# A transformer block with its backward pass: transposes by DMA in place of TensorE, the first norm remade, statistics and affine steps on ScalarE, under a new instruction order

## The chip, the cores and the metric

The kernel runs on one core of a Trainium2 chip. The metric is the device time of one execution in microseconds (us). Three runs of the kernel before took 559.96, 557.95 and 559.55 us, median 559.55. Separately, one execution was profiled; its span, from the first to the last instruction, is 557.1 us.

## The reference

A pre-norm block on 2048 rows of 512 bfloat16 values: windowed attention (32 heads of 16, eight keys per query at distances 0, 2, ..., 14), a residual, a second norm, a feed-forward network of width 1792 with tanh-gelu, a residual. Output is the forward result and the gradients of seven inputs.

```python
qkv = (x @ wqkv)                      # norm(x) comes in as x
idx = pos[:, None] - off[None, :]     # off = 0, 2, ..., 14
logits = einsum("bhsd,bhswd->bhsw", q, k[idx]) * scale   # masked where idx < 0
o = einsum("bhsw,bhswd->bhsd", softmax(logits), v[idx])
h  = x + o @ wo
h2 = h + gelu(norm(h) @ w1 + b1) @ w2 + b2
# returned: h2, and vjp(grad_out) for x, wqkv, wo, w1, b1, w2, b2
```

## The kernel before

The 2048 rows are worked on in four chunks (c = 0 to 3) of 512 rows. Tiles are held in two layouts: token-major (rows on partitions) and feature-major (features on partitions); much of the work beside the matmuls is turning one into the other. TensorE can turn a 128x128 block with a matmul against an identity, whose result in PSUM must be evicted; the DMA engines can turn a whole 512x512 tile with a transposing transfer.

**Forward attention, per chunk** (`p1_ln` to `p1_h`). The first norm (`layernorm`, line 330) is taken, stored to DRAM (`ln1st`, line 579) and turned. q, k and v are projected; q and k come out feature-major. VectorE multiplies q with eight shifted k (`dots`, line 450), TensorE sums over a head, softmax follows. For the value sum, and later for the gradients, q, k, v and the gradient `go` must lie token-major in DRAM, so that a strided load, the *gather* (line 438, issued on GpSimd's queue), can fetch 18 neighbouring rows per partition. For k and q, `to_tm_store` (line 410) makes that copy: per half chunk, eight transposes on TensorE, one eviction by ScalarE, one store of 256 KB. `band` (line 487) multiplies gathered rows by coefficients on VectorE, sums on TensorE (line 502) and evicts on ScalarE (line 507), four times per chunk. Its token-major result is turned back by `turn` (line 511: eight transposes, one eviction; twice per chunk) or, for the pairs listed in `FMB` and `FMO`, by `turned` (line 522: one transposing DMA of 512 KB, from SBUF to SBUF). Then come `wo`, the residual (line 716), the second norm and its DMA turn.

**Feed-forward and its gradient, per chunk** (`p2_h`, `p2_out`, `p2_dg`, `p2_bwd`). 56 products of 4 matmuls per direction; ScalarE evicts and takes gelu, square and tanh, VectorE makes the gelu's derivative. The norm's gradient is `ln_bwd` (line 530): a scaled eviction with a sum on ScalarE, a reduction (line 539) and an affine step `u` (line 541) on VectorE, then two additions.

**Attention gradients, per chunk** (`p3_go`, `p3_dots`, `p3_bands` for q, v, k, `p3_gl1`). Three gathers and three bands per chunk; their results, turned, meet the transposed weights in `p3_gl1` (line 950), where the stored first norm is loaded again in permuted rows (line 941) for the norm's gradient. **Weight gradients** (`wg_ffn`, line 976) are matmuls over all rows, spread by the order over the second half as filler.

**What sets the order.** Each function registers operations through `op`, numbered as they are registered, with the buffers that they read and write. Nothing runs in that order: `emit` (line 118) issues the operations as the list `ORDER` (line 1182) says, by number, and each engine's program, SP's and GpSimd's DMA queues among them, is that list cut to the engine. An engine runs its program strictly in turn, so an instruction that waits holds all that stand behind it on the same engine. `HOMES` (line 1267) gives each buffer its SBUF address or PSUM bank. Two buffers at one address may not be live together, so a home adds waits too. Both lists were written by a planner ahead of time, which knew an estimated duration for each operation (the second argument of `op`).

## Time and profile before

| | before |
|---|---|
| median of three runs | 559.55 us |
| span of the profiled execution | 557.1 us |
| TensorE matmuls busy | 537.7 us (97%) |
| VectorE busy | 493.4 us (89%) |
| ScalarE busy | 314.7 us (57%) |
| GpSimd busy | 36.2 us (7%) |
| granted TensorE clock | 0.999 |
| moved by DMA | 126.65 MB, 227 GB/s in the mean |

The profiled execution's own time is not listed beside its span; the runs' median stands 2.45 us above the span.

A row that names a line, an engine and an operation gives the tile written and those read, the shapes, how often it ran (x64), then the busy time of the group, the mean of one in nanoseconds, and the engine's idle time ahead of it with what ended that. Busy time of TensorE merges overlapping matmuls, and each matmul's duration includes its way through the pipeline, so that the busy time of a short group is longer than what it delays the next. Rows of stretches ("82.00:196.00") give the length, then for PE (TensorE), PEld (its weight loads), DVE (VectorE), ACT (ScalarE) and POOL (GpSimd) the busy time and number of instructions, the granted clock, the mean busy share of the 16 DMA engines (which can exceed 1 when two queues interleave) and the bytes moved. In a row with a start, a duration and an engine, SPq is SP's DMA queue.

### The profile page before, as it was taken

To read this page: it belongs to the slowest core of one execution; us is meant where nothing else is said; L and a number is where in the kernel's file an instruction comes from. 1 tells how busy PE (TensorE), PEld (TensorE's weight loads), DVE (VectorE), ACT (ScalarE), POOL (GpSimd) and SP (SyncE) were. 2 spreads that over 40 slices of the span, in tenths; PEclk is the share of its full clock that TensorE was granted. 3 is DMA by queue.
4 is the path that set the end of the run, shared out by engine and by line. 5 is a ranking of instruction groups with operands and counts; after the bars stand their busy time and mean duration, and the time that the engine had idled before them with its cause. 6 is when DMAs were issued, how large, how long until landed. Compare 5 with 4: busy or idle time off the path is not lost. (4 is left out here: it accounts for less than half of the span.)

```text
span 557.1 us, 8572 instructions
## 1 busy us (share of the span) xinstructions
PE 537.7 (97%) x3276; PEld 248.1 (45%) x3327; DVE 493.4 (89%) x652; ACT 314.7 (57%) x500; POOL 36.2 (7%) x55
## 2 busy tenths in 40 slices
PE   7899899999999999999999999999999998999996
PEld 3454453444444444444444444464444443444442
DVE  7989999999999999787777378999999798999983
ACT  3997489978899956664440324122155534462423
POOL 1210010030000000002000000000011100010000
PEclk9999999999999999999999999999999999999999
DMA  8699979999688245589899988999999999887954
GB/s 253 180 276 269 350 199 375 259 224 284 172 210 241 62 122 132 114 167 244 161 201 187 204 170 188 247 222 245 197 328 286 390 264 377 287 339 165 243 126 130
DMA packets 199674, 126.65 MB, mean 227 GB/s; under 512 B 152081, under 2 KB 193233, under 8 KB 195537
## 3 DMA queue, kind: packets, MB, share of 16 engines
q1 hardware_dynamic: 194016, 84.68, 64.7%
q0 software_dynamic: 5616, 41.42, 20.1%
q8 instruction: 26, 0.43, 0.3%
q14 instruction: 16, 0.12, 0.1%
HBM read 55.74 MB, written 35.21 MB: 163 GB/s over the span
## 5 line engine op out<-in xcount | busy, mean ns | idle before, releaser
L823 PE MATMUL ps<-goT,w2T 128*128 128x512 bf16 x224 | 53.1, 379 | 0.4 <-DVE xb L825 0.2
L279 ACT CAST wgs<-ps 128x512 bf16<-128x512 f32 (+1 forms) x30 | 16.5, 563 | 64.8 <-PE ps L976 51.5
L741 PE MATMUL ps<-ln2T,w 128*128 128x512 bf16 x224 | 52.4, 379 | 0.2
L837 PE MATMUL ps<-w1T,xb 128*128 128x512 bf16 x219 | 50.9, 379 | 0.2
L795 PE MATMUL ps<-w,gl 128*128 128x512 bf16 x217 | 50.6, 379 | 0.4
L743 ACT ACTIVATE xb<-ps,b1c 128x512 bf16<-128x512 f32 x56 | 35.9, 693 | 19.1 <-PE ps L741 18.9
L950 PE MATMUL ps<-wqkvT,gqkvT 128*128 128x512 bf16 x186 | 44.1, 379 | 0.4 <-issue 0.2
L825 DVE SCALAR_TENSOR_TENSOR xb<-xb,ps 128x512 bf16<-128x512 bf16 x56 | 36.6, 682 | 7.3 <-PE ps L823 6.6
L976 PE MATMUL ps<-gor,gw2in 128*128 128x512 bf16 x164 | 39.2, 379 | 0.3 <-issue 0.2
L976 PE MATMUL ps<-gw1in,ln 128*128 128x512 bf16 (+1 forms) x185 | 38.9, 352 | 0.4
L493 DVE TENSOR_TENSOR prbk<-Rk,cfk 128x4096 bf16<-128x4096 bf16 x16 | 35.7, 2286 | 3.1 <-DMA Rk<-q_d 2.5
L493 DVE TENSOR_TENSOR prbq<-Rq,cfq 128x4096 bf16<-128x4096 bf16 x16 | 35.9, 2286 | 2.9 <-PE ps L502 2.0
L493 DVE TENSOR_TENSOR prbv<-Rv,cfv 128x4096 bf16<-128x4096 bf16 x16 | 35.7, 2280 | 2.9 <-DMA Rv<-go_d 2.0
L454 DVE TENSOR_TENSOR prb<-got,vw 128x4096 bf16<-128x4096 bf16 x16 | 36.0, 2273 | 1.6 <-ACT got L279 1.6
L493 DVE TENSOR_TENSOR prbo<-Ro,cfo 128x4096 bf16<-128x4096 bf16 x16 | 35.9, 2284 | 0.1
L454 DVE TENSOR_TENSOR prf<-qt,kt 128x4096 bf16<-128x4096 bf16 x16 | 35.9, 2277 | 0.0
L976 PEld LDWEIGHTS <-ln 128*128 128x128 bf16 x256 | 24.1, 98 | 25.2 <-issue 4.1
L823 PEld LDWEIGHTS <-w2T 128*128 128x128 bf16 x224 | 21.9, 98 | 27.4 <-issue 1.4
L837 PEld LDWEIGHTS <-xb 128*128 128x128 bf16 x224 | 21.9, 98 | 26.4
L795 PEld LDWEIGHTS <-gl 128*128 128x128 bf16 x224 | 21.8, 98 | 26.4 <-issue 0.4
L741 PEld LDWEIGHTS <-w 128*128 128x128 bf16 x224 | 21.4, 98 | 26.5 <-issue 2.5
L599 PE MATMUL ps<-ln1T,wqk 128*128 128x512 bf16 x127 | 30.0, 379 | 1.3 <-DMA wqk<-in_A_wqkv_dram 1.0
(174 smaller groups left out, 962.0 us busy)
## 6 DMA issues: line engine op xcount, KB each, us to landing
Ro<-v_d POOLq DMA_DIRECT2D x4, 1280.0 KB, 9.4
Rq<-k_d POOLq DMA_DIRECT2D x4, 1280.0 KB, 8.9
Rv<-go_d POOLq DMA_DIRECT2D x4, 1280.0 KB, 5.9
Rk<-q_d POOLq DMA_DIRECT2D x4, 1280.0 KB, 6.6
g_d<-gl SPq DMA_DIRECT2D x9, 512.0 KB, 3.7
gh_d<-xb SPq DMA_DIRECT2D x9, 512.0 KB, 4.2
Ro<-v_d POOLq DMA_DIRECT2D x4, 1024.0 KB, 7.3
Rq<-k_d POOLq DMA_DIRECT2D x4, 1024.0 KB, 8.3
```

Source lines behind the costliest of these rows:

```text
L279: fn = lambda: A.copy(out=ap(), in_=pap())
L454: op("DVE", tt_us(4096), lambda g=g, pr=pr: V.tensor_tensor(out=pr(), in0=ql()[:, g, :].unsqueeze(1).to_broadcast([P, W, 512]), in1=_sub(k ...
L493: V.tensor_tensor(out=pr().rearrange("p a j (d h) -> p a j d h", h=H), in0=_sub(R()[:, o0, 0:1], [[st, 2], [512, 4], [32, DH], [1, H]]), i ...
L599: T.matmul(ps()[:, gg * 512:(gg + 1) * 512], lhsT=wq_()[:, dc, sel * D + g * P:sel * D + (g + 1) * P], rhs=cols(st_[c]["ln1T"], dc, c in F ...
L741: T.matmul(ps(), lhsT=w1()[:, dc, f * P:(f + 1) * P], rhs=cols(ln2T[c], dc, c in FM2), start=(dc == 0), stop=(dc == DC - 1))
L743: op("ACT", act_us(512, 1), lambda f=f, ps=ps, xb=xb, f0=f0: A.activation(out=xb()[:, f - f0, :], in_=ps(), func=ACT.Identity, bias=b1c[:, ...
L795: T.matmul(ps(), lhsT=d["g"][f // 4]()[:, f % 4, j * P:(j + 1) * P], rhs=w2()[:, f, :], start=(f == 0), stop=(f == FT - 1))
L823: T.matmul(ps(), lhsT=w2T()[:, dc, f * P:(f + 1) * P], rhs=cols(goT, dc, True), start=(dc == 0), stop=(dc == DC - 1))
L825: op("DVE", 0.61, lambda f=f, ps=ps, z=z, f0=f0: V.scalar_tensor_tensor(out=z()[:, f - f0, :], in0=z()[:, f - f0, :], scalar=1.0, in1=ps() ...
L837: T.matmul(ps(), lhsT=d["d"][f // 4]()[:, f % 4, j * P:(j + 1) * P], rhs=w1T()[:, f, :], start=(f == 0), stop=(f == FT - 1))
L950: T.matmul(ps(), lhsT=gT()[:, j, b * P:(b + 1) * P], rhs=wqkvT()[:, k0 + b, :], start=(i == 0 and b == 0), stop=(i == 2 and b == 3))
L976: T.matmul(ps()[:, 0:N], lhsT=l, rhs=r, start=(n == 0), stop=(n == k - 1))
```

## The change

- **q and k copies** (`FMS = ("q", "k")`). `to_tm_store` is no longer called for them. `fm_store` writes each chunk feature-major to a new DRAM tensor (four stores of 128 KB). `fm_turn`, registered after the feed-forward's weights, reads it back by a transposing DMA and stores it token-major.
- **Turns** (`FMB` for all twelve, `FMO = (2, 3)`). The nine pairs that still used `turn` in the gradients (seven) and in the output of chunks 2 and 3 (two) use `turned`.
- **First norm** (`LX`). It isn't stored. In `p3_gl1` x is loaded in permuted rows and the norm is made again by 16 affine steps on ScalarE; for that the mean times the scale travels with the scale through the small DRAM detour (`rstdp` has twice the columns).
- **Second norm's statistics** (`S2A`). The residual add becomes an add with a running sum; per row tile ScalarE scales that sum and takes a square with a sum, in place of VectorE's two statistics instructions.
- **Norm gradients** (`UA`). `u` goes from VectorE to ScalarE.
- **`wo` transposed** (`WOD`). A DRAM-to-DRAM copy with permuted rows, then one transposing DMA, in place of a transposing DMA and a copy on GpSimd.
- Zero rows are stored from the warm-up's zero tile; two small memsets go.
- `ORDER` and `HOMES` are new throughout.

```diff
+    def fm_store(fm, off, n, c):
+        for g in range(4):
+            store(f_d[n][c], lambda g=g: _ap(f_t[n][c][8 * g:8 * g + 1, :], [[CH, 8], [H * CH, DH], [1, CH]]), fm, lambda g=g: fm()[:, g, off:off + CH], 128,
+                  key=g, skey=g // 2, tag="fst" + n)
+    def fm_turn(n, c, dst, back):
+        st = sb("ft" + n, [P, 4, D])
+        r = c * CH + (RPAD if back else 0)
+        xload(st, lambda: st(), lambda: f_t[n][c][:], 512, r=[f_d[n][c]], tag="fx" + n)
+        store(dst, lambda: dst()[r:r + CH, :].rearrange("(a p) d -> p a d", p=P), st, lambda: st(), 512, key=(c, 0), tag="tmst" + n)
...
+                if sq:
+                    jk = sb("jks", [P, D])
...
+                    op("ACT", 0.12, lambda t=t: A.mul(mv[:, t, 0:1], st[:, t, 0:1], -1.0 / D), r=[(ST, t)], w=[(MV, (t, 0))], tag="smean" + tag)
+                    op("ACT", act_us(D, 1, True), lambda t=t, j=j, jk=jk: A.activation(out=jk(), in_=src()[:, j, :], func=ACT.Square, bias=mv[:, t, 0:1],
+                                                                                       accum_out=mv[:, t, 1:2]),
...
-        store(ln1_d[c], lambda: ln1_d[c]()[:].rearrange("(j p) d -> p j d", p=P), ln1, lambda: ln1(), 512, tag="ln1st")
+        if not LX:
+            store(ln1_d[c], lambda: ln1_d[c]()[:].rearrange("(j p) d -> p j d", p=P), ln1, lambda: ln1(), 512, tag="ln1st")
...
+        if tag in UA:
+            op("ACT", act_us(D, 2), lambda: A.activation(out=u()[:, j, :], in_=xhap(), func=ACT.Identity, scale=sx_[:, i:i + 1], bias=c0_[:, i:i + 1]),
+               r=[xh, (SX, i), (C0, i)], w=[(u, j)], tag="u" + tag)
...
+            elif c in S2A:
+                op("DVE", 0.61, lambda j=j, ps=ps: V.tensor_tensor_reduce(out=h()[:, j, :], in0=ps(), in1=xt()[:, j, :], scale=1.0, scalar=0.0, op0=ALU.add,
+                                                                          op1=ALU.add, accum_out=st2[:, c * TPC + j, 0:1]),
...
+        if LX:
+            xr = sb("xr", [P, TPC, D])
...
+                op("ACT", act_us(D, 2), lambda t=t, j=j: A.activation(out=ln1()[:, j, :], in_=xr()[:, j, :], func=ACT.Identity,
+                                                                     scale=rstdp[:, t:t + 1], bias=rstdp[:, NT + t:NT + t + 1]), r=[xr, RP], w=[(ln1, j)], tag="nx")
...
+    if WOD:
+        op("SP", 0.5, lambda: SY.dma_start(out=wop_t[:], in_=_ap(A_wo, [[D, DH], [DH * D, H], [1, D]])), w=[WOP], dma=512 / DMA_RATE, tag="wop", mode=4)
...
-FMO = ()
-FMB = (('q', 3), ('v', 3), ('k', 3), ('k', 2), ('v', 2))
+FMO = (2, 3)
+FMB = tuple((n, c) for n in 'qvk' for c in range(4))
...
+FMS = ("q", "k")
+WOD = True
+LX = True
+S2A = (0, 1, 2, 3)
+S1A = ()
+UA = ("1", "2")
```

More of the change, by code (lines that the diff above doesn't have):

```diff
@@ L333, in layernorm @@
             acc = per == 1 and g0 in STA
+            sq = c in S2A if tag == "2" else per > 1 and c in S1A
             for j in js:
@@ L358, in layernorm @@
             else:
[L359 removed]
+                op("DVE", 0.08, lambda s=s, sq=sq: V.tensor_scalar(out=ve[:, s], in0=mv[:, s, 1], scalar1=1.0 / D if sq else EPS, scalar2=EPS if sq else None, op0=ALU.mult if sq else ALU.add,
+                                                                   **({"op1": ALU.add} if sq else {})),
                    r=[(MV, t) for t in ts], w=[(VE, k)], tag="ve" + tag)
@@ L646, in p1_qkv @@
         for fm, o, dd, back, n in ((kt, PAD, k_d, True, "k"), (qt, 0, q_d, False, "q")):
-            (tm_dma if (n, c) in TMD else to_tm_store)(fm, o, dd, c, back, n, c not in QKP)
+            if n in FMS:
+                fm_store(fm, o, n, c)
+            else:
+                (tm_dma if (n, c) in TMD else to_tm_store)(fm, o, dd, c, back, n, c not in QKP)
     def p1_attn(c):
```

79 lines of the change are left out of this document (51 added, 28 removed), and 240 rows, old and new, of tables (HOMES, ORDER).

## The prediction

> **What bounds the kernel now.** I read the page's first lines, then the busy time by stage, then the instructions around the first feed-forward matmul, then the chain that ended last.
>
> ```profile
> span 557.1 us, 8572 instructions
> ...
> PE 537.7 (97%) x3276; PEld 248.1 (45%) x3327; DVE 493.4 (89%) x652; ACT 314.7 (57%) x500; POOL 36.2 (7%) x55
> ```
>
> TensorE is nearly never idle, but the share is a mean. I cut the span where its character changes: the first feed-forward matmul (82), the end of the stretch with ScalarE full (196), the attention gradients under way (336), weight-gradient matmuls alone (546):
>
> ```profile
> core 0: us, PE busy (x) PEld busy (x) DVE busy (x) ACT busy (x) POOL busy (x), PEclk, DMA share, GB/s
> 0.00:82.00 82.00, 73.25 (x550) 36.00 (x558) 76.89 (x109) 60.04 (x82) 10.94 (x19) 1.00 0.87 256
> 82.00:196.00 114.00, 112.84 (x633) 50.97 (x641) 112.40 (x167) 106.84 (x135) 7.11 (x8) 1.00 0.84 229
> 196.00:336.00 140.00, 139.12 (x636) 63.21 (x646) 107.39 (x216) 63.83 (x111) 3.89 (x1) 1.00 0.83 170
> 336.00:546.00 210.00, 205.74 (x1432) 95.03 (x1454) 194.08 (x159) 82.27 (x171) 14.28 (x27) 1.00 0.89 260
> 546.00:557.10 11.10, 6.73 (x32) 2.84 (x29) 2.63 (x5) 1.76 (x4) 0.00 (x0) 0.94 0.41 118
> ```
>
> After 82 us TensorE is idle for 1.2 + 0.9 + 4.3 us before the tail: there the time is TensorE's stream, and only fewer matmul columns shorten it. The head is different. VectorE works 76.9 of 82 us, while TensorE has only projections and attention and leaves 8.8 us. What lets the feed-forward in is chunk 0's second norm:
>
> ```profile
> 72.88 0.15 DVE L364 SCALAR_TENSOR_TENSOR nm<-mv,rstd 128x4 f32<-128x4 f32 x1
> 73.14 2.93 ACT L369 ACTIVATE ln<-h,nm,rstd 128x512 bf16<-128x512 bf16 x4
> 76.09 1.89 SPq L273 DMA_TRANSPOSE ln2T<-ln  x1
> ...
> 81.92 0.81 PE L741 MATMUL ps<-ln2T,w 128*128 128x512 bf16 x3
> ```
>
> So VectorE's queue decides when `nm` comes (72.9), and the first feed-forward matmul follows 9 us later.
>
> **TensorE's part of the change.** All k and q transposes for the token-major copies (16 groups of 8) leave TensorE, and so do 18 `turn` groups: 14 of the gradients and 4 of chunks 2 and 3 of the attention output. That is 34 x 8 = 272 transposes. Their price is read from the chain, not from the groups' busy time:
>
> ```profile
> 478.49 0.89 PE ps L518 x16
> ...
> 543.23 9.51 PE ps L976 x44
> ```
>
> ```profile
> L419 PE MATMUL ps<-Pmat,kt 128*128 128x128 bf16 x64 | 4.9, 219 | 0.6 <-ACT tmv L279 0.6
> L419 PE MATMUL ps<-Pmat,qt 128*128 128x128 bf16 x64 | 4.7, 219 | 1.8 <-DVE h L716 1.0 <-ACT tmk L279 0.7
> ...
> L518 PE MATMUL ps<-ident,gqs 128*128 128x128 bf16 x48 | 3.7, 219 | 0.0
> ```
>
> Sixteen in a row move the chain 0.89 us, 0.0556 us each; the group's 0.075 us (4.9/64) holds a pipeline tail under which the next matmul already runs. 272 x 0.0556 = 15.1 us. Of these, the 128 k/q transposes all stand ahead of the first feed-forward matmul in the old order, so they lie in the head, and 144 (8.0 us) behind it. The new list also lets two band sums and one row sum (about 1.4 us) that stood ahead of that matmul come after it. So the stream behind it is shorter by 8.0 - 1.4 = 6.6 us. This saving is nearly certain if nothing else becomes the bound.
>
> **VectorE's and ScalarE's part.**
>
> ```profile
> L454 DVE TENSOR_TENSOR prf<-qt,kt 128x4096 bf16<-128x4096 bf16 x16 | 35.9, 2277 | 0.0
> ...
> L347 DVE BATCH_NORM_STATS2 st<-h 128x6 f32<-128x512 bf16 x16 | 10.8, 674 | 0.0
> ...
> L539 DVE CUSTOM_DVE_ANT_0 jk<-gyr,ln1b 128x512 bf16<-128x512 bf16 x16 | 10.7, 684 | 2.3 <-ACT gyr L536 2.3
> ...
> L716 DVE TENSOR_TENSOR h<-ps,xp 128x512 bf16<-128x512 f32 x16 | 10.5, 675 | 0.0
> ...
> L541 DVE TENSOR_SCALAR u<-ln1b,sx,c 128x512 bf16<-128x512 bf16 x16 | 6.3, 407 | 0.5
> ...
> L348 DVE BATCH_NORM_AGGREGATE mv<-st 128x2 f32<-128x6 f32 x32 | 5.8, 182 | 1.1
> ...
> L658 DVE TENSOR_REDUCE mx<-ps 128x128 bf16<-128x1024 f32 x4 | 4.8, 1208 | 0.0
> ...
> L676 DVE RECIPROCAL r<-ps 128x128 bf16<-128x128 f32 x4 | 3.7, 940 | 0.6 <-PE ps L671 0.6
> ```
>
> ```profile
> L279 ACT COPY gqkvT<-ps 128x1024 bf16<-128x1024 bf16 x14 | 14.1, 1014 | 7.9 <-PE ps L518 7.7
> L369 ACT ACTIVATE ln<-h,nm,rstd 128x512 bf16<-128x512 bf16 x16 | 11.9, 805 | 1.0 <-DVE nm L364 1.0
> L536 ACT ACTIVATE gyr<-ps,rstdp 128x512 bf16<-128x512 f32 x16 | 11.0, 687 | 22.9 <-PE ps L950 22.8
> ...
> L279 ACT COPY tmk<-ps 128x1024 bf16<-128x1024 bf16 x8 | 8.1, 1034 | 0.2 <-PE ps L419 0.2
> ...
> L538 ACT ACTIVATE c<-sg 128x1 f32<-128x1 f32 x32 | 5.9, 201 | 0.3
> ...
> L536 ACT ACTIVATION_READ_ACCUMULATOR gyr<-ps,rstdp 128x1 f32 x16 | 3.2, 198 | 0.0
> ```
>
> VectorE loses 16 x (0.674 + 0.182) = 13.7 us of second-norm statistics and 32 x 0.407 = 13.0 us of `u`. The residual add becomes an add with a sum; the nearest row with a sum is the custom reduction at 0.684, so +0.01 to +0.1 each. Net about -25 us. ScalarE loses 16 x 1.03 + 18 x 1.01 = 34.7 us of evictions. It gains 48 affine steps (32 `u`, 16 remade norms) x 0.805 = 38.6 us and 16 squares with a sum at 0.687 + 0.198 + 0.201 (the small scaling) = 1.09, so 17.4 us. Net +21, to 336 us, 62% of the span: no bound on the whole.
>
> In the head the list matters more than the sums. Counting what stands on VectorE ahead of chunk 0's `nm`: the old list has 12 products of q and k, 3 maxima, 3 reciprocals and 4 pairs of second-norm statistics; the new one 10, 1, 1 and none. That is 4.6 + 2.4 + 1.9 + 3.4 = 12.3 us, with the small ones about 13, so `nm` could come at 60 instead of 73. Against that, the new list puts a softmax exponent of chunk 2 on ScalarE between the first and the other three norms, and that exponent waits for a maximum that stands after `nm`. The head's gain lies between 0 and 13 us; I take 6.7, the middle, since the norm is released early and then partly held.
>
> **The DMA part.** Each k and q chunk goes out feature-major (4 stores of 128 KB in place of 2 of 256 KB), is read back transposed and stored again: 8 transposes and 8 stores of 512 KB more. 9 more `turned` transposes (2 for the output, 7 for gradients). 4 stores of the first norm go; its 16 loads become loads of x; the `wo` detour adds one copy and trades one transpose for another.
>
> ```profile
> 56.00:70.00 14.00, 12.31 (x130) 6.30 (x130) 13.90 (x17) 6.94 (x8) 0.54 (x1) 1.00 0.99 351
> ...
> 182.00:196.00 14.00, 13.87 (x64) 6.36 (x65) 13.73 (x26) 13.97 (x14) 1.03 (x1) 1.00 0.22 68
> 196.00:210.00 14.00, 13.70 (x63) 6.05 (x62) 13.86 (x28) 7.24 (x8) 0.00 (x0) 1.00 0.41 99
> 210.00:224.00 14.00, 13.95 (x66) 6.37 (x65) 13.90 (x29) 9.10 (x14) 0.00 (x0) 1.00 0.52 131
> 224.00:238.00 14.00, 13.95 (x66) 6.36 (x65) 11.05 (x18) 10.87 (x21) 0.00 (x0) 1.00 0.61 125
> 294.00:308.00 14.00, 13.95 (x65) 6.37 (x65) 10.45 (x32) 2.76 (x8) 0.00 (x0) 1.00 1.07 185
> ```
>
> The last of these windows holds nearly only transposes: 185 GB/s x 14 us = 2.59 MB, 4.9 of 512 KB, in 1.07 x 14 = 15 us of all engines, so 3.0 us each. The first holds plain traffic: 4.9 MB in 13.9 us, 1.5 us per 512 KB. The change adds 17 x 3.0 + 8 x 1.5 + 1.5 - 4 x 1.5 = 59 us of DMA. The k and q detour is 36 us of it; priced at 0.216 us a matmul (9.51/44), TensorE's stream in the new list stands at 124 to 200 us where they are issued, and in the old run the clock is some 28 us ahead of the stream (82 against 54 at the first feed-forward matmul). So it is the stretch from 152 to 228, whose last windows have 0.78 + 0.59 + 0.48 + 0.39 of 14 us free, 31 us; its readers, the k and q gathers, stand 110 us further on in the list. I cost it at nothing; without that cover it would press on the 0.83 to 0.89 of the later stages.
>
> The 7 gradient transposes add 21 us to the stage 336:546, whose DMA share is 0.89 x 210 = 187 us: 208 of about 203 us. That is over 1, yet 294:308 ran at 1.07 with TensorE busy 13.95 of 14. SP pays 1.9 us for each (the `ln2T` row), behind which it holds x loads, weight-gradient loads and stores; it has room:
>
> ```profile
> SPq L273 <- DVE prbv L493: 17.3, 1, 17.3
> ```
>
> The `wo` copy on GpSimd (3.9 us) falls in a stage with VectorE idle a quarter of the time: nothing.
>
> **Sum.** 557.1 - 6.6 (stream) - 6.7 (head) = 543.8 us of span. The median of the runs, 559.55, stands 2.45 above the profiled span, so 546 us.
>
> **The rivals.**
>
> Half the engines: each new k or q store walks its destination with an outermost size of 8. If a DMA is spread over no more engines than that, the 20 stores listed ahead of the first feed-forward matmul take 20 x 0.25 x 1.5 x 2 = 15 us on half the engines, which at the head's 0.87 have only 11 free; ln2's transpose then queues and the head stays: 557.1 - 6.6 + 2.45 = 553 us. For it: the head's windows reach 0.99. Against: the removed stores (8 of 256 KB and 4 of 512 KB) give back 12 us on all engines. [...] Chance 0.09.
>
> ScalarE bounds 82:196, where it works 106.8 of 114 us. The stage gains 12 squares (13 us) and about 4 `u` (3), and loses some 6 evictions (6): 117 us in a stage that should itself shrink. If gelus and evictions wait for that, it costs 3 to 8 us: about 552. Against: the next stage has ScalarE at 64 of 140, and its tanh and squares can be late. Chance 0.09.
>
> Gathers late, and slower than before: TensorE's one large gap in the last stage is a k band behind its gather.
>
> ```profile
> 472.50 0.61 PE L502 MATMUL ps<-prbk,S 128*32 128x512 bf16 x8 [1.73 <-DVE prbk L493]
> ```
>
> ```profile
> DVE prbk L493 <- DMA Rk<-q_d: 2.5, 2, 1.6
> ```
>
> With 21 us more of transposes on the engines that carry the gathers, each of the 12 q, v and k gathers could open such a gap: 12 x 1.73 = 21, so 546 + 21 = 567 us. From 7 such gaps on the result is no change, from 10 slower. Against: today only two waits of this kind exist, with windows over 1.0. Chance 0.14, 0.08 of it slower.
>
> The whole head gain: `nm` at 60 and nothing holds the norms: 557.1 - 6.6 - 13 + 2.45 = 540 us. Chance 0.12.
>
> [...]
>
> **How the numbers follow.** Forecast 0.56 (its own range 542 to 551), rivals 0.09, 0.09, 0.14, 0.12. The range 538.5 to 555 holds all but the late gathers and the edges. Within 0.5% (what a measurement of this kernel can't tell from no change) is 556.8 to 562.4. Faster 0.86, same 0.06, slower 0.08.
>
> **What would show it.** TensorE busy 520 to 524 us; no `tmk`, `tmq`, `gqkvT` evictions; first `ln2T` matmul at about 75 us (82: the head stayed; 69: all of it); DMA share above 0.5 in the stretch 150 to 230; no new gaps ahead of `prbk`, `prbv`, `prbq`. Wrong if TensorE's idle time after the first feed-forward matmul exceeds 20 us, or if ScalarE is full up to 200 us with TensorE waiting for `xb`.

## The result, and the profile after

The changed kernel took 554.15 us (median of 4 runs, 551.92 to 555.12); the kernel before, on the same chip, took 558.97 us (4 runs, 557.95 to 559.96). The ratio is 0.9908, 95% interval 0.9886 to 0.9930: faster by 0.9%, more than the 0.5% that the prediction takes for no change. The forecast was 546.0, with a range of 538.5 to 555.0. So the direction came true and the range held, but only 4.8 of the 13 us arrived. (Of the runs further down one, 557.99 us of x9, lies over 1.5% above that kernel's fastest and is left out of its ratio.)

The first lines of the page of the changed kernel: span, busy time, the granted clock in 40 slices, and SyncE's DMA queue.

```profile
span 553.3 us, 8162 instructions
...
PE 530.4 (96%) x3055; PEld 233.8 (42%) x3055; DVE 473.0 (85%) x606; ACT 334.3 (60%) x564; POOL 34.8 (6%) x54
...
PEclk8989999899999999999999999999999999999999
...
q1 hardware_dynamic: 232592, 96.26, 76.2%
```

VectorE lost 20.4 us (forecast 25) and ScalarE gained 19.6 (forecast 21). TensorE has 272 matmuls fewer by its weight loads (3327 before, 3055 now), as counted, but its busy time is 530 and not 520 to 524. The clock row is new: three early slices show an 8 where the kernel before had only nines. The queue q1 takes 76.2% of 553.3 us where it had 64.7% of 557.1: 61 us more, the forecast 59.

The same stages as before:

```profile
core 0: us, PE busy (x) PEld busy (x) DVE busy (x) ACT busy (x) POOL busy (x), PEclk, DMA share, GB/s
0.00:82.00 82.00, 73.59 (x438) 31.30 (x439) 72.87 (x101) 53.77 (x84) 13.30 (x19) 0.96 0.85 246
82.00:196.00 114.00, 107.42 (x588) 46.00 (x587) 105.09 (x150) 102.86 (x147) 5.36 (x7) 0.99 0.98 249
196.00:336.00 140.00, 140.00 (x662) 63.13 (x660) 99.43 (x205) 83.62 (x142) 1.94 (x1) 1.00 1.06 223
336.00:546.00 210.00, 208.38 (x1369) 93.09 (x1368) 195.56 (x153) 93.06 (x193) 14.23 (x27) 1.00 0.95 271
```

From 196 us on TensorE is as full as before. In 82:196 it is idle for 6.6 us, where it was idle for 1.2 (and that number of before includes holes: its trace lacks 51 matmul records over the whole span). The DMA share in that stage rose from 0.84 to 0.98, and in the next from 0.83 to 1.06, with SyncE's queue q1 alone at 105.8% there: a share above 1 needs no second queue.

TensorE's own rows show where (start, duration, operation, number, and in brackets the idle time ahead with what ended it):

```profile
75.92 2.75 PE L784 MATMUL ps<-ln2T,w 128*128 128x512 bf16 x12 [0.45 <-DMA ln2T<-ln]
...
92.99 1.90 PE L748 MATMUL ps<-wo,oT 128*128 128x512 bf16 x8 [0.86 <-DMA oT<-ost]
...
100.28 4.03 PE L838 MATMUL ps<-w,gl 128*128 128x512 bf16 x11 [2.15 <-DMA w<-in_B_w_dram]
...
161.22 1.89 PE L748 MATMUL ps<-wo,oT 128*128 128x512 bf16 x8 [2.00 <-ACT xb L786]
```

The first feed-forward matmul (L784) starts at 75.92, forecast "about 75". The head has what was promised. But the last matmul ends at 547.06 (552.73 before), so behind the first feed-forward matmul TensorE needs 471.1 us, and before it needed 470.8. The 6.6 us that left its stream were paid back in full.

SyncE's queue and ScalarE at the places that these rows point to:

```profile
70.16 3.16 SPq L277 DMA_TRANSPOSE ln2T<-ln  x1
...
85.99 4.96 SPq L277 DMA_TRANSPOSE oT<-ost  x1
91.06 0.52 SPq L268 DMA_DIRECT2D w<-in_B_w_dram  x1
...
540.49 8.37 SPq L273 DMA_DIRECT2D out_dram<-gx  x13
548.96 1.09 SPq L273 DMA_DIRECT2D out_dram<-wgsq  x2
```

```profile
159.54 1.06 ACT L804 ACTIVATE x<-xb 128x1024 bf16<-128x1024 bf16 x1 [3.60 <-DMA oT<-ost]
```

Three things are to be seen. The new transfer that turns chunk 2's attention output waits at the head of SyncE's queue until its data are there (85.99) and is then issued for 4.96 us; the load of w2 stands behind it and lands 2.15 us too late. The transfer that turns chunk 3's output stops ScalarE for 3.60 us: the cast of a pre-activation has a home on top of the tile that is still being turned. And at the end SyncE issues 13 gradient stores in a row, so the last weight gradients leave at 548.96, while the last matmul ended at 547.06; from that matmul to the end it is 6.2 us, before 4.4.

The account of the forecast's span of 543.8 against 553.3: head +0.7 (75.92 for 75.2), the stretch from the first feed-forward matmul to the last +6.9 (471.1 for 464.2), the end +1.9.

### The profile page after: what moved, and what is told of

It reads as the page before. It is cut to its first block, busy times and chain, and to the rows that moved or that the text cites. A ratio compares the mean times of both kernels' runs of the same rounds, so it can differ in the third digit from the quotient of the medians.

```text
span 553.3 us, 8162 instructions
## 1 busy us (share of the span) xinstructions
PE 530.4 (96%) x3055; PEld 233.8 (42%) x3055; DVE 473.0 (85%) x606; ACT 334.3 (60%) x564; POOL 34.8 (6%) x54
## 3 DMA queue, kind: packets, MB, share of 16 engines
q1 hardware_dynamic: 232592, 96.26, 76.2%
## 4 chain that ended last, share of the span: by engine, by line
PE 76%; DMA 8%; issue 6%; ACT 4%; DVE 3%; SPq 1%; POOL 1%; DVEq 0%; POOLq 0%
PE ps L1028 26%; PE ps L838 8%; PE ps L784 8%; PE ps L880 8%; PE ps L866 8%; PE ps L1002 7%; PE ps L533 5%; PE ps L904 2%; DMA gqkvT<-gqs 2%; DMA w<-in_B_w_dram 2%; DVE prf L485 2%; DMA gqkvT<-gks 2%; PE ps L493 1%; DMA wqk<-in_A_wqkv_dram 1%; PE ps L635 1%
## 5 line engine op out<-in xcount | busy, mean ns | idle before, releaser
L838 PE MATMUL ps<-w,gl 128*128 128x512 bf16 x224 | 54.0, 389 | 2.1 <-DMA w<-in_B_w_dram 2.1
L880 PE MATMUL ps<-w1T,xb 128*128 128x512 bf16 x224 | 52.6, 379 | 0.7 <-DVE xb L868 0.7
L784 PE MATMUL ps<-ln2T,w 128*128 128x512 bf16 x224 | 52.3, 379 | 0.7 <-DMA ln2T<-ln 0.5
L635 PE MATMUL ps<-ln1T,wqk 128*128 128x512 bf16 x128 | 32.6, 401 | 2.4 <-DMA ln1T<-ln 2.3
L784 PEld LDWEIGHTS <-w 128*128 128x128 bf16 x224 | 21.4, 98 | 28.4 <-issue 3.8
```

The lines of the kernel that those rows point to most:

```text
L635: T.matmul(ps()[:, gg * 512:(gg + 1) * 512], lhsT=wq_()[:, dc, sel * D + g * P:sel * D + (g + 1) * P], rhs=cols(st_[c]["ln1T"], dc, c in F ...
L784: T.matmul(ps(), lhsT=w1()[:, dc, f * P:(f + 1) * P], rhs=cols(ln2T[c], dc, c in FM2), start=(dc == 0), stop=(dc == DC - 1))
L838: T.matmul(ps(), lhsT=d["g"][f // 4]()[:, f % 4, j * P:(j + 1) * P], rhs=w2()[:, f, :], start=(f == 0), stop=(f == FT - 1))
L880: T.matmul(ps(), lhsT=d["d"][f // 4]()[:, f % 4, j * P:(j + 1) * P], rhs=w1T()[:, f, :], start=(f == 0), stop=(f == FT - 1))
```

## The experiments

Five theories stood to be told apart, the later ones formed as the earlier fell short. **A, single transfers**: a few late transfers stop TensorE at named places. **B, volume**: the DMA engines are full, and whatever is taken away only moves the wait. **C**: chunk 3's turned output stops ScalarE. **D**: the transfer that turns chunk 0's normed rows is the new bound of the head. **Clock**: TensorE's clock is halved after an idle time (in the changed kernel's profile 0.50 from 101.2 to 104.6 us, behind the 2.15 us ahead of the w2 product). The runs come from several chips, on which the kernel before has medians of 557.4 to 559.0 us, so ratios say more than medians. In the diffs the shift of the two written-out lists is left out.

The table holds one profiled execution of each kernel, read from TensorE's rows: start of the first feed-forward matmul, TensorE's idle time just ahead of it, the stretch from there to the last matmul, the idle time in that stretch, the 3.41 us pieces of half clock in it, and the time from the last matmul to the end.

| run | first | idle ahead | stretch | idle in it | half clock | end | median, ratio to the kernel before [95%] |
|---|---|---|---|---|---|---|---|
| changed kernel | 75.9 | 0.45 | 471.1 | 8.2 | 1 | 6.2 | 554.15, 0.9908 [0.9886, 0.9930] |
| x1_out_turn_pe | 77.6 | 2.98 | 472.2 | 7.8 | 1 | 5.1 | 557.12, 0.9994 [0.9969, 1.0018] |
| x2_w2_ahead | 77.1 | 2.85 | 477.4 | 12.4 | 4 | 6.3 | 561.8, 1.0063 [1.0040, 1.0085] |
| x3_store_16 | 73.9 | 1.27 | 473.7 | 9.4 | 2 | 6.2 | 552.79, 0.9881 [0.9840, 0.9922] |
| x4_grad_turn_pe | 75.6 | 3.78 | 475.7 | 6.8 | 2 | 5.1 | 559.55, 1.0026 [1.0002, 1.0050] |
| x5_c2_unturned | 75.4 | 2.88 | 469.2 | 9.2 | 1 | 5.8 | 553.74, 0.9930 [0.9905, 0.9955] |
| x6_one_store | 76.0 | 1.98 | 472.7 | 11.1 | 2 | 5.9 | 551.75, 0.9903 [0.9877, 0.9929] |
| x7_tail_pool | 76.0 | 4.23 | 469.1 | 9.3 | 1 | 4.4 | 553.66, 0.9926 [0.9902, 0.9951] |
| x8_fill | 77.8 | 3.05 | 469.2 | 7.7 | 1 | 5.3 | 553.57, 0.9922 [0.9896, 0.9948] |
| x9_scalar_order | 77.3 | 4.29 | 467.3 | 4.5 | 1 | 5.7 | 552.31, 0.9884 [0.9861, 0.9907] |
| x10_best | 77.4 | 3.63 | 469.2 | 5.6 | 1 | 4.5 | 552.89, 0.9927 [0.9903, 0.9952] |
| x11_stats_dve | 76.9 | 0.95 | 467.8 | 6.7 | 0 | 6.3 | 555.31, 0.9950 [0.9932, 0.9968] |
| x12_kq_pe | 91.7 | 0.28 | 467.8 | 5.5 | 1 | 5.9 | 565.95, 1.0121 [1.0086, 1.0155] |
| x13_ln2_turn_pe | 74.0 | 0.27 | 466.0 | 4.7 | 0 | 5.4 | 548.13, 0.9837 [0.9804, 0.9870] |
| x14_all | 73.7 | 0.27 | 464.4 | 2.5 | 0 | 4.4 | 546.69, 0.9806 [0.9782, 0.9830] |

Single executions of one kernel differ by 2 to 8 us here (x2 561.0 to 562.6, x5 550.3 to 558.0), so a fix worth 2 us is hardly seen in the median. Nor does one profile's stretch show it: x7 has the changed kernel's list unaltered and differs only in four stores at the end, and its stretch is 2.0 us shorter. What a profile does show is whether a certain wait at a certain place is there or gone.

**x1: the outputs of chunks 2 and 3 back on TensorE.**

```diff
-FMO = (2, 3)
+FMO = ()
```

> The changed kernel with the attention output of chunks 2 and 3 turned by TensorE again (32 transposes, 4 evictions, two DMA transposes less); all else as changed. Theory A (the shorter stream was eaten between 84 and 182 us by the turned outputs: three waits of wo for oT, 0.86 + 2.00 + 0.63 us, and w2 issued behind oT on SP, a wait of 2.15 us and 1.7 us of half clock): these 7.3 us go, 32 x 0.056 = 1.8 us come back, so about 548.5 us against 554.15 changed and 558.97 before, and no wait of the feed-forward's second matmul for w2. Theory B (the DMA engines are simply full, at a share of 0.97 of the span): two transposes out of 90 make no difference, 554 to 556 us.

The ratio is 0.9994. The waits on `oT` by DMA went, and another took their place:

```profile
99.35 0.89 PE L748 MATMUL ps<-wo,oT 128*128 128x512 bf16 x2 [3.53 <-ACT xb L786]
```

The evictions that come back with the transposes stood on ScalarE ahead of a gelu and of evictions of pre-activations, and `wo` waits for the PSUM banks of these. Theory A's 548.5 is missed, but the run can't refute it either: undoing one part in a list made for the other brings stalls of its own.

**x2: the w2 load one place earlier on SyncE**, ahead of chunk 2's turning transfer.

> The changed kernel with the load of w2 moved one place on SP, ahead of chunk 2's turned output. Theory A: SP held w2 from 79 to 91 us behind a transpose that waited for its source; w2 lands before its first matmul, 2.15 us of wait and 1.7 us of half clock go, but the turned output lands later and wo waits 1 to 3 us more: 551 to 553 us. Theory B: w2 and the transpose share full engines, whichever goes first: 554 us.

Slower, 1.0063, where both theories had expected 554 or less. The two transfers changed places, and so did the wait:

```profile
100.44 3.59 PE L748 MATMUL ps<-wo,oT 128*128 128x512 bf16 x8 [7.29 <-DMA oT<-ost]
```

The turned output now comes behind 1792 KB of weights, and `wo` waits 7.29 us for it. In both orders tried, at least one of the two transfers is late.

**x3: the feature-major stores of q and k with 128 as the outermost size**; the features arrive permuted, so the attention gradients mix heads.

```diff
-            store(f_d[n][c], lambda g=g: _ap(f_t[n][c][8 * g:8 * g + 1, :], [[CH, 8], [H * CH, DH], [1, CH]]), fm, ...
+            store(f_d[n][c], lambda g=g: f_t[n][c][g * P:(g + 1) * P, :], fm, ...
```

> The changed kernel with the feature-major k and q stores writing their 128 rows one after the other (outermost size 128 in place of 8), so that the features lie in another order in the copy and the gradients are those of mixed heads: only the walk of the store changes. Rival R1 (a store with outermost size 8 runs on half the engines): the 32 stores take half as long, the head and the stretch to 175 us get shorter by several us, 549 us or less. Theory A: the waits hang on what stands on SP ahead of w2 and oT, 553 to 555 us.

0.9881 [0.9840, 0.9922] against 0.9908: no difference that can be told, and the rival's 549 us aren't reached. The walk with an outermost size of 8 isn't what kept most of the gain away. Something does set these stores apart, though: on one semaphore with 39 transfers, six of them such stores, the changed kernel's trace holds 582 = 33 x 16 + 6 x 9 landing events, nine for each of these stores and sixteen for each of the others. On how many engines they ran, no run shows. And x3's head is the shortest of those that turn the normed rows by DMA (73.9 us, the others 75.4 and more); one profile can't tell whether that is the walk.

**x4: five of the seven gradient turns back on TensorE** (q and v of chunks 0 and 1, k of chunk 0: 80 transposes).

```diff
-FMB = tuple((n, c) for n in 'qvk' for c in range(4))
+FMB = tuple((n, c) for n in 'qvk' for c in (2, 3)) + (('k', 1),)
```

> The changed kernel with five of the twelve gradient turns (q of chunks 0 and 1, v of 0 and 1, k of 0) by TensorE again: 80 transposes and 10 evictions more, five DMA transposes less in the stage 336 to 546. Theory A: TensorE's stream is the bound there, 80 x 0.056 = 4.4 us more, 558.5 us. Theory B (DMA is the bound): 15 us of DMA less, 554 us or below.

The ratios 1.0026 and 0.9908 are 1.2% apart, 6.6 us, where 80 x 0.0556 = 4.4 us was worked out for the transposes alone. The stretch is 4.6 us longer. In the last stages TensorE's stream is the time. The stage of the attention gradients in x4, for the row of the changed kernel above:

```profile
336.00:546.00 210.00, 206.72 (x1419) 94.94 (x1417) 190.72 (x148) 99.12 (x198) 14.24 (x27) 1.00 0.87 254
```

The DMA share is 0.87 in place of 0.95, and TensorE gets nothing for it: 50 more matmuls in the same 210 us, and the rest comes later.

**x5: chunk 2's output not turned at all** (`wo` reads the untransposed tile, so the forward result is another).

```diff
-        if c in FMO:
+        if c == 2:
+            d["oT"] = ost
+        elif c in FMO:
             turned(ost, oT, "o")
```

> The attention output of chunk 2 is not turned at all: the four projections of chunk 2 read the tile as it stands, so the result is not that of the reference; everything else, places in the list included, is as in the changed kernel. Theory A (single late transfers): this one transpose holds SyncE until its output is ready and 4.96 us more, so TensorE waits 0.86 us for it and 2.15 us for the w2 load behind it, and pays 1.7 us of half clock after the second wait. Without it both idle times and the half clock go: 554.2 - 4.7 = 549.5 (549 to 551). Theory B (the volume): the DMA engines are full from 84 to 336 us (share 0.98 to 1.06), so that what is taken away here only moves the wait to the next transfer: 552.5 to 555, with the idle time of TensorE between 84 and 196 us still above 4 us.

Both waits of theory A went, as it says:

```profile
98.68 4.48 PE L840 MATMUL ps<-w,gl 128*128 128x512 bf16 x19 [0.47 <-DVE st L757]
```

The stretch is 469.2 us, no shorter than x7's 469.1, and the median of 12 runs, 553.74, shows nothing of the expected 549.5. The profile has what stands against it: TensorE waits 2.88 us ahead of the first feed-forward matmul, where the changed kernel's profile has 0.45, and then runs 3.41 us at half clock. Theory A has the place right and isn't the whole. (The 0.45 is not the rule either: x7, with the same list, has 4.23 us there and the same start of 76.0. In the changed kernel's profile two pieces of half clock, at 9.0 and 36.3 us, had made TensorE itself later, by an estimated 2 x 1.7 = 3.4 us.)

**x6: q and k stored once, feature-major, into the arrays that the gathers read**; the eight turning transfers and eight stores are left out, and the attention gradients are those of other numbers.

```diff
-            store(f_d[n][c], lambda g=g: _ap(f_t[n][c][8 * g:8 * g + 1, :], [[CH, 8], [H * CH, DH], [1, CH]]), fm, lambda g=g: fm()[:, g, off:off + CH], 128,
...
+            store(dst, lambda g=g: dst()[r + g * P:r + (g + 1) * P, :], fm, lambda g=g: fm()[:, g, off:off + CH], 128,
...
-            if n in FMS:
-                fm_turn(n, c, dd, n == "k")
+            pass
```

> Queries and keys are stored once, straight into the arrays that the gathers of the backward read, feature-major as they are; the eight turning transfers and the eight stores behind them are left out (so the gradients of attention are those of other numbers). This takes 36 us of DMA time and 16 SyncE issues away and adds no work elsewhere. The prediction costed the detour at nothing: 554 +- 1. Theory A: the idle times at 92 and 98 us lie ahead of the detour and stay; only those at 159 to 173 us (3.3 us) and part of those behind 430 us can go: 551 to 553. Theory B (volume): with 36 us fewer the engines are no longer full between 150 and 230 us, and the idle time of TensorE behind the head falls from 8.2 to below 4 us: 549 to 550.5.

0.9903 against 0.9908. The share of the DMA engines in 140:230 fell from 0.99 (changed kernel, first row) to 0.68 (x6, second fence), and the time stayed:

```profile
140.00:230.00 90.00, 86.48 (x421) 38.36 (x421) 82.11 (x144) 75.70 (x100) 2.47 (x2) 1.00 0.99 234
```

```profile
140.00:230.00 90.00, 85.00 (x411) 37.88 (x415) 81.42 (x140) 75.61 (x100) 2.48 (x2) 1.00 0.68 167
```

So theory B falls for this stretch: with 28 us of the engines free again, TensorE's idle time from the first feed-forward matmul on was not below 4 us but 11.1. The detour of q and k costs nothing that these runs can tell, as predicted. What full engines do to a single transfer in the head is another matter (x9).

**x7: chunk 0's four gradient stores on GpSimd's queue.**

```diff
-GXP = ()
+GXP = ((0, 0), (0, 1), (0, 2), (0, 3))
```

> Only the four stores of chunk 0's input gradient go out on GpSimd's queue instead of SyncE's. Theory: the end of the changed kernel is set by SyncE, which issues 13 of these stores in one row for 8.37 us and comes to the last weight-gradient stores at 548.96 though their evictions ended at 547.7; four stores fewer are 2.6 us, so the last store is issued at once behind its eviction: -1.3 us, 552.9 in time, and the stretch from the last matmul to the end falls from 6.2 to 4.9 us. Rival: the landing of the stores sets the end, not their issue: no change (554.2), stretch 6.2 us.

The step did what it should: SyncE's row is 1.65 us shorter (6.72 us for 8.37), and the time from the last matmul to the end is 4.4 us, as in the kernel before. x10 and x14, which have the same edit, show 4.5 and 4.4; the runs without it show 5.1 to 6.3.

```profile
538.42 6.72 SPq L273 DMA_DIRECT2D out_dram<-gx  x9
545.25 1.09 SPq L273 DMA_DIRECT2D out_dram<-wgsq  x2
```

The median (553.66) is not able to show 1.8 us.

**x8: ten matmuls whose results nobody reads, in each of two idle times** (ahead of chunk 3's queries, and ahead of the last group of chunk 0's second product, shown here).

```diff
+            def fill():
+                for _ in range(NFILL):
+                    T.matmul(pf(), lhsT=wo()[:, 0, 0:P], rhs=wo()[:, 0, :], start=True, stop=True)
```

> Ten matmuls of 128x512 on weights that lie there (their results are never read) are put into TensorE's queue at two places where it stood idle for 2.27 and 2.15 us: ahead of chunk 3's queries and ahead of the last group of chunk 0's second feed-forward product. Theory (clock): the half clock at 36.3 to 39.7 and 101.2 to 104.6 us follows an idle time of over 2.1 us; with the idle time filled the granted clock stays 1.00 there and two times 1.7 us are saved: 550.8 in time (550 to 552), and the mean clock goes from 0.989 to 0.995. Rival: the drop comes from something else than the idle time, or the transfers that TensorE waits for set the next step: 553.5 to 555, with drops at the same places.

At 98 to 105 us the wait is filled, there is no half clock, and the real matmuls follow without a gap:

```profile
100.49 2.32 PE L843 MATMUL ps<-wo 128*128 128x512 bf16 x10
102.65 3.62 PE L852 MATMUL ps<-w,gl 128*128 128x512 bf16 x15
```

But x7 has no half clock at this place either, without filling: its wait there was 1.19 us. So the filling is not shown to have saved the clock. A half clock came at 78.5 us, behind an idle time of 3.05 us ahead of the first feed-forward matmul; the stretch is 469.2, like x7's, and the median stayed at 553.57. The expected 550.8 missed: the drop at 36 us lay in the head, whose end something else sets.

**x9: one ScalarE instruction moved.** The cast (operation 793) that writes over chunk 3's attention output stands 27 places later.

```diff
-    ..., 733, 615, 793, 675, 720, ...
+    ..., 516, 735, 793, 758, 744, ...
```

> One instruction is moved: the cast of the third quarter of chunk 1's pre-activations (x <- xb on ScalarE, ready early) goes 27 places later in the list, behind two evictions of the first feed-forward product. In the changed kernel it is written over the memory of chunk 3's attention output, so it waits 3.60 us for the transfer that turns that output, and ScalarE's evictions wait behind it, and TensorE's projections behind these (idle 2.00, 0.63 and 0.68 us at 159 to 174 us). Theory C (the turned output of chunk 3 stops ScalarE, not the DMA volume): the three idle times go, 3.3 us, 554.2 - 3.3 = 550.9. Rival: the projections wait for the turned output itself, which lands at 159.5 us, and the idle time stays: 554.

```profile
77.31 4.44 PE L784 MATMUL ps<-ln2T,w 128*128 128x512 bf16 x12 [4.29 <-DMA ln2T<-ln]
...
160.46 2.76 PE L748 MATMUL ps<-wo,oT 128*128 128x512 bf16 x12 [1.02 <-DMA oT<-ost]
```

Of 2.00 + 0.63 + 0.68 us of idle time at 159 to 174 us, 1.02 is left, now on the transfer itself. Theory C holds: the waits for `xb` that stand there in the changed kernel and in x5, x6, x7, x8 and x11 are gone. The stretch is 467.3, 1.8 us below x7's; the median, 552.31, stays above the expected 550.9. The first row is the other half of the story: with the rest of the head in time, TensorE stands idle for 4.29 us ahead of the first feed-forward matmul. Why, VectorE and SyncE of the same run show:

```profile
62.57 0.16 DVE L382 SCALAR_TENSOR_TENSOR nm<-mv,rstd 128x4 f32<-128x4 f32 x1 [0.93 <-POOL rstd L379]
```

```profile
67.71 7.42 SPq L277 DMA_TRANSPOSE ln2T<-ln  x1
```

Chunk 0's `nm` comes at 62.6, 10.3 us earlier than in the kernel before (72.88), but the transfer that turns the normed rows is issued for 7.42 us (before: 1.89) and the first matmul follows the start of its issue by 9.6 us (before: 5.8). What it meets stands on GpSimd's queue (q0; SyncE's is q1). Two gathers (`Ro`) are issued as soon as `rstd` is done, and from 66 to 72 us their packets keep the engines busy for 88.0%:

```profile
62.54 1.12 POOL L475 DMA_DIRECT2D Ro<-v_d  x2
```

```profile
q0 software_dynamic: 225, 1.88, 88.0%
q1 hardware_dynamic: 247, 0.16, 18.9%
```

In the kernel before, this transfer had the engines nearly to itself (76 to 80 us):

```profile
q1 hardware_dynamic: 2081, 0.53, 69.0%
q0 software_dynamic: 15, 0.01, 0.7%
```

In the changed kernel's profile the transfer is issued at 70.16 us, with the two gathers at work; their last packet ends at 73.48, and the first feed-forward matmul comes 2.4 us after it (75.92). So the head's end seems to hang on the gathers, which stand right behind the same norm's `rstd` on GpSimd. No run moved them: this is read from the traces and not tested.

**x10: x9, x7, and chunk 2's output by TensorE, placed anew.**

> Three edits together: the move of x9, the four stores of chunk 0's input gradient on GpSimd's queue (x7), and chunk 2's attention output turned by TensorE again (16 transposes, two evictions on ScalarE, placed where the output is ready), chunk 3's still by DMA. Theory: behind the first feed-forward matmul nothing waits for a transfer any more until 449 us; from the changed kernel's 554.2: -3.3 (chunk 3), -0.86 - 1.2 to 2.15 (chunk 2 and w2) + 0.9 (16 transposes), -1.3 to -1.8 (end), and no half clock behind the head: 547 to 549, ratio to the kernel before 0.980 to 0.985. Rival (waits only move on, volume): 552 to 554.

0.9927, no better than x9 alone, where 0.980 to 0.985 was expected. As in x1 the returned eviction fell in a bad place, behind a table load and a gelu:

```profile
96.77 1.02 PE L784 MATMUL ps<-ln2T,w 128*128 128x512 bf16 x4 [2.60 <-ACT oT L283]
```

```profile
92.61 1.28 ACT L789 ACT_TABLE_LOAD   x1
93.91 1.91 ACT L789 ACTIVATE gl<-xb 128x2048 bf16<-128x2048 bf16 x1
95.72 0.99 ACT L283 COPY oT<-ps 128x1024 bf16<-128x1024 bf16 x1
```

So the removal of a late transfer is worth nothing here when it puts evictions on a full ScalarE.

**x11: the statistics of chunk 0's second norm back on VectorE.**

```diff
-S2A = (0, 1, 2, 3)
+S2A = (1, 2, 3)
```

> Only the statistics of chunk 0's second norm go back from ScalarE to VectorE (four pairs of the two statistics instructions in the places of the squares on ScalarE; the sum that the residual add delivered is dropped). The prediction's head term: VectorE's queue ahead of this norm sets the first feed-forward matmul. By it VectorE has about 4 x 0.8 = 3 us more ahead of the norm, and the first feed-forward matmul comes 2 to 3 us later (78 to 79 us for 75.9): 556 to 557 in time. Rival (the head ends with the transfer that turns the normed rows, or with TensorE's own queue, whichever engine did the statistics): 554, first matmul at 75.5 to 76.5 us.

```profile
65.47 0.16 DVE L382 SCALAR_TENSOR_TENSOR nm<-mv,rstd 128x4 f32<-128x4 f32 x1 [0.93 <-POOL rstd L379]
```

```profile
76.86 0.38 PE L784 MATMUL ps<-ln2T,w 128*128 128x512 bf16 x1 [0.95 <-DMA ln2T<-ln]
```

`nm` comes 2.9 us later than in x9, and yet the first feed-forward matmul isn't later than x9's 77.31. In these profiles VectorE's queue no longer decides the head; what it gained beyond some 8 us went into the wait for the transfer. The ratio is less clear: 0.9950 [0.9932, 0.9968] is 0.4% above the changed kernel's, so a part of the 2 to 3 us that the prediction's view asks for may be there.

**x12: q and k turned by TensorE again, in the changed order** (128 transposes, 16 evictions).

```diff
-FMS = ("q", "k")
+FMS = ()
```

> Queries and keys are turned by TensorE again in the changed kernel's order: 128 transposes and 16 evictions on ScalarE come back, the 32 feature-major stores, the 8 turning transfers and the 8 stores behind them go (16 stores come in their place). 128 x 0.0556 = 7.1 us of TensorE, nearly all ahead of or around the first feed-forward matmul; 36 us of DMA time less. Prediction (the detour costs nothing, and these transposes are worth their TensorE time only where TensorE is the bound): first feed-forward matmul 0 to 4 us later, behind it +3.5 us at most: 556 to 560. Rival (volume: the detour's 36 us of DMA cost as much as they save): 553 to 555.

Slower than both, 1.0121, and slower than the 556 to 560 us expected: the first feed-forward matmul comes at 91.7 us, 15.8 us later. One wait of 5.2 us in it is of this run's own making (a returned eviction behind others on ScalarE):

```profile
39.80 1.86 PE L653 MATMUL ps<-wv,ln1T 128*128 128x512 bf16 x4 [5.23 <-ACT tmk L283]
```

Behind the first feed-forward matmul the stretch (467.8) isn't longer than in the changed kernel. The turned copies of q and k are thus worth their detour in the head; how much of the 15.8 us is their due and how much the placing is open.

**x13: x9, and chunk 0's normed rows turned by TensorE** between the two halves of chunk 3's last value projection.

```diff
-FM2 = (0, 1, 2, 3)
+FM2 = (1, 2, 3)
```

> On top of x9, chunk 0's second normed rows are turned by TensorE (16 transposes, two evictions on ScalarE in the middle of chunk 3's projections) instead of by a transfer. In x9 the rows were ready at 67.7 us, SyncE issued their transfer for 7.42 us and the first feed-forward matmul waited 4.29 us, until 77.3. Theory D (the head is now bound by this transfer): first feed-forward matmul at 74 to 75 us, no idle time of over 1.5 us ahead of it and no half clock behind it; 16 x 0.0556 = 0.9 us more of TensorE are in this already: 552.3 - 2.3 to 3.3 - up to 1.7 = 548 to 550. Rival (VectorE's bands or the weights' load set the start): first matmul at 76 to 78 us, 552 to 554.

```profile
71.38 1.05 PE L413 MATMUL ps<-ident,ln 128*128 128x128 bf16 x16 [0.24 <-ACT tmv L283]
72.27 1.03 PE L653 MATMUL ps<-wv,ln1T 128*128 128x512 bf16 x4
...
74.01 1.02 PE L784 MATMUL ps<-ln2T,w 128*128 128x512 bf16 x4 [0.27 <-ACT ln2T L283]
```

548.13 us, ratio 0.9837 [0.9804, 0.9870], below x9's interval, though the two intervals just touch. The first feed-forward matmul comes at 74.0 with TensorE at work up to it, and no half clock follows. Theory D holds.

**x14: x13, x7, and five filling matmuls ahead of the w2 product.**

> x13 with two more edits: chunk 0's four gradient stores on GpSimd's queue (as in x7) and five filling matmuls (1.08 us, their results not read) ahead of the last group of chunk 0's second feed-forward product. If the account closes: x13's time less 1.0 to 1.8 us at the end and 0 to 1.7 us of half clock: 546 to 549, mean clock 0.996 or more, ratio to the kernel before 0.977 to 0.984. If the causes do not add up: as x13, or above 550.

```profile
span 542.4 us, 8209 instructions
...
PE 526.6 (97%) x3076; PEld 234.1 (43%) x3076; DVE 472.4 (87%) x606; ACT 336.4 (62%) x566; POOL 37.9 (7%) x58
...
PEclk9999999999999999999999999999999999999999
```

546.69 us (544.5 to 548.96), ratio 0.9806 [0.9782, 0.9830]: faster than both kernels, and all expectations met. On this chip the kernel before has a median of 557.36, so 10.7 of the forecast's 13 us are there, 1.5 of them from a head shorter than forecast (73.7 for 75.2). The stretch from the first feed-forward matmul to the last is 464.4 us, with 1.1 us of filling matmuls and 2.5 us of idle time in it; the forecast had said 470.8 - 6.6 = 464.2. The account closes: against the changed kernel's profile -2.2 (head), -6.8 (stretch), -1.9 (end) = -10.9 us, and the spans are 553.3 and 542.4.

## Why the prediction was right or wrong

**The stream: mechanism and size right, and it was not the end of the matter.** 272 weight loads fewer, 15.1 us; behind the first feed-forward matmul 6.6 us (there the trace counts 144 transposes fewer and 24 small sums more). x14, with the stalls removed, has the stretch at 464.4 us for the forecast 464.2, and x4 shows that transposes in the last stages cost their full time. The step that failed stands behind it: "This saving is nearly certain if nothing else becomes the bound", and then in the sum, -6.6 with nothing against it. The waits that the change's own transfers make in the stage 82:196 took it back: 0.86 and 2.15 us (chunk 2's output and the w2 load behind it; gone in x5), an estimated 1.7 us (3.41 x 0.5) of half clock behind them, and some 3 us where chunk 3's output stopped ScalarE (x9).

**"It has room": the step that was wrong.** The working looked at SyncE's longest wait, 17.3 us in the last stage, and let that stand for the whole queue. It priced two of the added transfers, the outputs of chunks 2 and 3, at 3.0 us of the engines each and never as a wait of the one who reads them. A turn on TensorE takes 0.45 us for eight transposes (8 x 0.0556) and 1.01 us for their eviction (`gqkvT` in the kernel before). It also priced 1.9 us of SyncE for each gradient turn; in the changed kernel's trace the twelve take 1.6 to 9.3 us. A turn by DMA held SyncE until the data were there and then for that time more (chunk 2's output: until 85.99 us and then 4.96 us); what stands behind it is named in the list, and was not looked up. Nor were the homes: that the cast on ScalarE lies over the tile being turned is written in them.

**The head: right in size, 6.0 us for 6.7, and in part by luck.** VectorE's queue did release `nm` early: at 65.02 us in the changed kernel's profile and at 62.57 in x9's, for 72.88 before (the working had "could come at 60"). The earlier of the two has the later first feed-forward matmul, 77.31 us for 75.92. In the changed kernel's profile, from `nm` to the issue of the transfer it is 5.1 us, before 3.2: that is the exponent, as the working says. GpSimd's `rstd`, ahead of `nm`, took 3.00 us, before 1.04; why is open. The step that the working lacks is the transfer behind the norms, whose 5.8 us from issue to first matmul were carried over from the kernel before. They are 5.8 in the changed kernel's profile, where the norms came late, but 9.6 in x9 and 6.3 in x11: in x9 the two gathers have the engines at 88.0% from 66 to 72 us, and an `nm` 2.5 us earlier than the changed kernel's bought nothing more. That the transfer waits for the gathers is the author's reading, not tested. The 6.7 us were the middle of 0 to 13 and not the price of this.

**The end: a term set at zero.** The span behind the last matmul was taken as unchanged; with 13 gradient stores in one row ahead of the last weight gradients it grew by 1.9 us, and x7 gave it back.

**From span to time: 0.6 us too much.** The working added 2.45 us, a median against one profile's span; in the runs of the changed kernel the time stands 1.8 us above the span of the same execution (555.12 and 553.3).

**The clock: not foreseen.** TensorE busy for 520 to 524 us was forecast, 530.4 were measured; three pieces of half clock of 3.41 us in the profile, an estimated 1.7 us each, are 5.1 of it, of which 1.7 behind the head.

**The DMA part: right.** The volume came as worked out (61 us for 59), the stretch of 150 to 230 us filled up (0.99 in 140:230), and "I cost it at nothing" for the detour holds (x6).

**The rivals.** Half the engines (0.09): each such store lands with nine events in place of sixteen (the changed kernel's trace), but no run shows its engines, and its price isn't seen; x3 changes the walk, and the changed kernel's ratio lies within x3's interval. ScalarE as the bound of 82:196 (0.09): it works 102.9 of 114 us, and TensorE does wait for `xb` there, but the cause is one instruction in the wrong place (x9), not the sum; the time that this rival gave, 552, was nearer than the forecast, for another reason. Late gathers (0.14): TensorE waits for none of `prbk`, `prbv` and `prbq` in the changed kernel; in x4 it stops twice for 1.1 us ahead of such a band, both times for a returned eviction (`gqkvT`) and not for a gather. The whole head gain (0.12): `nm` came at 62.6 to 65.5 us (x9, the changed kernel, x11), and then the exponent and the transfer of the normed rows held it. The mark set for a wrong forecast, 20 us of idle time behind the first feed-forward matmul, was too wide: 8.2 sufficed.

By the runs, turning on TensorE was the better way where someone waits for the result (x13: the first feed-forward matmul at 74.0 us, with the transfer, in x9, at 77.3), and not where TensorE is the bound and nobody waits (x4: 80 such transposes make the stretch 4.6 us longer).

## What to carry to other kernels

A transfer that replaces work on the bound engine can cost nothing in volume (x6) and yet its whole gain in latency: for each one, look up who reads the result next, what stands behind it on the queue that issues it, and which buffers lie over its source. Move to DMA the turns that nobody waits for soon, and leave on the engine those at the start of a stage. When a chain is shortened by 10 us, the next link (here a transfer of 6 to 10 us) has to be priced anew under the new load, with what the other queue has under way at that time, not copied.

## What the runs showed of the hardware

In the changed kernel's profile the clock granted to TensorE was 0.50 in three pieces of 3.41 us, from 9.0, 36.3 and 101.2 us on, and 1.00 in the rest of 6 to 547 us; in the kernel before it was 1.00 from 6 us to the last matmul. Four pieces of the changed kernel, the second at half clock, by stretches (fields as in the stages above):

```profile
97.80:101.21 3.41, 1.26 (x7) 0.47 (x6) 3.37 (x8) 3.38 (x4) 0.00 (x0) 0.99 1.17 289
101.21:104.62 3.41, 3.41 (x10) 1.21 (x9) 3.32 (x3) 3.35 (x7) 0.00 (x0) 0.50 1.01 202
159.24:162.65 3.41, 1.43 (x7) 0.77 (x8) 1.13 (x4) 3.08 (x3) 0.00 (x0) 1.00 1.21 249
162.65:166.07 3.42, 2.79 (x14) 1.17 (x12) 2.29 (x7) 3.39 (x5) 0.00 (x0) 1.00 1.11 289
```

Behind 1.26 of 3.41 us busy the next piece had half clock, behind 1.43 it had not; the half clock at 36.3 us came behind 1.15 of 3.42 us busy, but the one at 9.0 behind 1.87 of 3.41. Nor does the idle time ahead of the first feed-forward matmul say it alone: behind 2.98 us in x1 and 2.85 in x2 the clock row shows no loss in that slice (a 9), behind 2.88 in x5 and 1.98 in x6 it shows an 8. What decides it, the runs don't show. Behind the 2.15 us in the changed kernel it cost an estimated 1.7 us more (3.41 x 0.5).

The runs of one kernel differ in the granted clock: those of the kernel before have a mean of 0.995 to 1.000, those of the changed kernel and of x1 to x14 0.982 to 0.999, and over 106 timed runs of these, each against the mean of its own kernel, a clock lower by 0.01 goes with 4.7 us more. Filling matmuls took the place of the wait in x8 and x14, and no half clock followed there; but x13's profile has none either, without filling.

A transposing transfer of 512 KB kept SyncE for very different times: the same one, of chunk 0's normed rows, took 1.89 us in the kernel before, 3.12 in x11, 3.16 in the changed kernel and 7.42 in x9. The traces point to the gathers on the other queue. In the kernel before their last packet ended 0.33 us after the start of the issue (76.42 for 76.09). In the changed kernel it ended 3.3 us after that start (73.48 for 70.16), and SyncE was held until 73.32; in x9 the gathers had the engines at 88.0% from 66 to 72 us, and SyncE was held from 67.71 to 75.13. No run changed the gathers alone.
